# First products of an attention and feed-forward kernel regrouped: q of four groups by token quarters, longer weight rows, a first tile in halves, and a new table of priorities

## The chip, the cores and the metric

One core of a Trainium2 chip runs the whole kernel. The metric is device time in microseconds (us) of one execution. A kernel is run several times and the median is quoted. With each run goes the mean granted clock of the TensorE (PE); 1.0 is full speed. The other engines are DVE (VectorE), ACT (ScalarE), POOL (GpSimd) and SP (SyncE, which issues the transfers).

A profile is one execution seen by the hardware profiler: for every instruction its start and duration, and for every idle stretch of an engine the instruction or transfer that ended it, as inferred from semaphore events. "Issue" is put down where an engine was idle and no semaphore that the profile shows was waited for.

## The reference, cut to what matters

One transformer block over 2,048 tokens of width 1,024 in bf16. The attention works in four segments of 512 tokens with a memory between them; the feed-forward part has 3,584 hidden columns.

```python
h  = x + A(layernorm(x))            # 32 heads of 32, four segments s = 0..3
#   per segment: p = softmax(q k^T * scale + mask);  o = g * memory part + (1-g) * p v
#                memory M += phi(k)^T v ;  z += sum phi(k)       (read by the later segments)
h2 = h + (silu(LN(h) w1) * (LN(h) w3)) w2
```

## The kernel before: the parts that matter here

The kernel is written as a graph of operations which a small list scheduler puts in order at build time, on each engine by class and then by sequence number. A table `SHIFT` moves each unit of work in that order. It has two numbers per unit and was tuned by search, so the order of every engine's list follows from it.

```python
def schedule(self):
    for o in ops:
        late, cls = SHIFT.get(o.unit, (0, 0))
        o.seq += late + 1e-6 * o.seq
        o.cls += cls
    ...                                  # list scheduling with estimated costs, PSUM banks as a resource
```

A dense product is a chain of matmuls of a 128x128 weight with up to 512 columns. Each is one weight load and one product in the PE's list.

```python
def mms(self, group, items, cls, split=4, eager=False):
    for i in range(0, len(items), split):
        part = items[i:i + split]
        def emit(e, gr, part=part):
            return [e.matmul(p[0](gr), p[1], p[2], start=p[3], stop=p[4]) for p in part]
        ...
def project(self, s, kind, half, i, w):          # q, k, v of segment s; 8 products of 512 columns
    ...
    self.mms(gr, items, 5)
```

The head of the program (`first_half`) loads tiles x0 to x3 of 128 tokens, normalises and transposes them, and multiplies them by the first half of wq and wk as they come, in quarters of 128 tokens:

```python
loads = [x0, x1, wq[:, :, 0:256], x2, x3, wk[:, :, 0:256], wq[:, :, 256:512], wk[:, :, 256:512], wv]   # shortened
work = [(w, i, Group([(5,), (6,), (7,), (4,)], safe=True)) for w in (wq, wk) for i in range(2)]
for c0 in range(0, 512, 128):
    for w, i, gr in work:
        self.mms(gr, [... 8 products of 128 columns ...], 5, split=4, eager=True)
```

At the end of each half segment, `finish` and `memory` issue runs of small matmuls: sums and weighted sums of the exponentials over 32-wide column tiles (`column`), and 64 products of 32x33 for the memory. A group of such matmuls lies between the dense products:

```python
# column(...):
for kc in range(4):
    for i in range(4):
        ins.append(e.matmul(ps[32*i:32*i+32, b*512 + 128*kc:(b+1)*512], lhsT(i, kc, j), at[i, kc][:, j, :],
                            tile_position=(0, 32 * i), ...))
# memory(...): 4 x 4 x 4 products
ins.append(e.matmul(ps[32*j:32*j+32, b+33*i:b+33*i+33], pkn[:, 4*i+kc, 32*j:32*j+32], v[:, kc, g0+i, j, 0:33], ...))
```

The softmax here doesn't subtract the row's maximum and nothing guards it: scores larger than these inputs give would overflow.

## Time and profile before

| | before |
|---|---|
| time, median of 3 runs (range) | 896.66 us (895.69 to 897.35) |
| span of the profiled run, clock | 895.0 us, 1.0 |
| PE busy, share of the span | 880.6 us, 98% |
| DVE / ACT / POOL busy, share | 47% / 32% / 19% |
| matmuls recorded, weight loads recorded | 5,833 / 5,921 |
| first scores begin | 20.76 us |

The share of busy time says which engine bounds; the chain of waits says where the remaining idle time is. The lines that carry this are shown in the prediction below.

### The profile page before, as it was taken

The numbers are of one execution on the slowest core, as the hardware profiler recorded it, in microseconds if no ns is written. First come the engines' busy times: TensorE is split into PE (matmuls) and PEld (weight loads), VectorE is DVE, ScalarE is ACT, GpSimd is POOL, SyncE is SP. The second block draws the span as 40 slices with busy tenths as digits, with TensorE's granted clock in tenths as the row PEclk, the third lists the DMA queues.
The fourth block names the chain that finished last, engine by engine and source line by source line (L and its number), as shares of the span: only waits on it lengthen the run. The fifth ranks groups of instructions, "written<-read, shape, count | busy, mean of one in ns | idle before, by whom it ended". The sixth has DMA issues, their size and how long they took to land.

```text
span 895.0 us, 13604 instructions
## 1 busy us (share of the span) xinstructions
PE 880.6 (98%) x5833; PEld 403.4 (45%) x5921; DVE 417.6 (47%) x631; ACT 287.9 (32%) x306; POOL 173.8 (19%) x226
## 2 busy tenths in 40 slices
PE   8999999999999999999999999999999999999998
PEld 5343444444444444444444444444444444444445
DVE  5784848585848485754555311211334333331111
ACT  6767766656565646111111100000111111110000
POOL 2553445353534343100200000000000000000000
PEclk9999999999999999999999999999999999999999
DMA  7899755634541221753475211113223221301110
GB/s 235 227 212 271 187 142 147 187 92 130 165 99 57 72 70 58 225 153 92 120 224 140 85 36 36 30 46 90 64 60 94 71 71 48 95 24 41 40 37 30
DMA packets 146540, 96.32 MB, mean 108 GB/s; under 512 B 45488, under 2 KB 133680, under 8 KB 146480
## 3 DMA queue, kind: packets, MB, share of 16 engines
q1 hardware_dynamic: 146480, 95.45, 38.8%
q8 instruction: 47, 0.77, 0.4%
q14 instruction: 13, 0.11, 0.0%
HBM read 76.55 MB, written 8.39 MB: 95 GB/s over the span
## 4 chain that ended last, share of the span: by engine, by line
PE 97%; issue 1%; DVE 1%; DMA 1%; ACT 0%; SPq 0%; ACTq 0%; DVEq 0%
PE ps L708 89%; PE ps L1107 4%; PE ps L1057 3%; DMA xs<-in_A_x_dram 1%; PE ps L985 0%; PE ps L1184 0%; ACT et L1069 0%; PE ps L1100 0%; DVE t L1260 0%; DVE hm L1265 0%; PE ps L720 0%; SPq L299 0%; DVE R L1163 0%; ACT sg L1257 0%; DVE Nsb L1171 0%
## 5 line engine op out<-in xcount | busy, mean ns | idle before, releaser
L708 PE MATMUL ps<-hnT,w1b 128*128 128x512 bf16 x876 | 218.4, 379 | 1.4 <-issue 0.3
L708 PE MATMUL ps<-hnT,w3b 128*128 128x512 bf16 x873 | 217.4, 379 | 1.5 <-issue 0.5
L1257 ACT ACTIVATE sg<-ps 128x512 bf16<-128x512 f32 x112 | 66.9, 597 | 403.1 <-PE ps L708 403.1
L708 PE MATMUL ps<-w2b,hm 128*128 128x512 bf16 (+1 forms) x907 | 195.3, 372 | 0.9
L1069 ACT ACTIVATE et<-ps 128x2048 bf16<-128x2048 f32 x80 | 150.0, 1875 | 39.3 <-PE ps L1057 38.9
L1260 DVE SCALAR_TENSOR_TENSOR t<-sg,ps 128x512 bf16<-128x512 bf16 x112 | 76.8, 685 | 169.4 <-ACT sg L1257 169.2
L708 PEld LDWEIGHTS ps<-w2b,hm 128*128 128x128 bf16 x924 | 90.4, 98 | 103.2
L708 PEld LDWEIGHTS ps<-hnT,w1b 128*128 128x128 bf16 x896 | 86.5, 98 | 105.5 <-issue 8.2
L708 PEld LDWEIGHTS ps<-hnT,w3b 128*128 128x128 bf16 x896 | 86.5, 98 | 105.4 <-issue 2.9
L1078 POOL TENSOR_SCALAR_AFFINE_SELECT et<-et 128x512 bf16<-128x512 bf16 x96 | 84.0, 881 | 126.2 <-ACT et L1069 126.0
L1265 DVE SCALAR_TENSOR_TENSOR hm<-t,ps 128x512 bf16<-128x512 bf16 x112 | 76.7, 686 | 50.5 <-PE ps L708 47.9
L1289 DVE TENSOR_TENSOR ob<-hr,ps 128x512 bf16<-128x512 bf16 (+1 forms) x33 | 22.1, 671 | 143.0 <-PE ps L708 143.0
L708 PE MATMUL ps<-wo,oT 128*128 128x512 bf16 x249 | 60.7, 380 | 0.6 <-issue 0.3
L708 PE MATMUL ps<-xnT,wp 128*128 128x512 bf16 (+1 forms) x345 | 59.7, 320 | 1.4 <-issue 0.6
L708 PE MATMUL ps<-hnT,wp 128*128 128x512 bf16 x250 | 59.0, 380 | 0.7 <-issue 0.6
L708 PEld LDWEIGHTS ps<-xnT,wp 128*128 128x128 bf16 x352 | 27.7, 98 | 26.9 <-issue 3.6
L708 PEld LDWEIGHTS ps<-wo,oT 128*128 128x128 bf16 x256 | 23.9, 98 | 29.8 <-issue 2.9
L708 PEld LDWEIGHTS ps<-hnT,wp 128*128 128x128 bf16 x256 | 23.6, 98 | 29.8 <-issue 3.8
L1200 POOL TENSOR_TENSOR oT<-Nsb,R 128x512 bf16<-128x512 f32 x23 | 35.8, 1569 | 4.1 <-DVE R L1197 4.1
L1163 DVE STREAM_TRANSPOSE R<-Rc 128x1024 f32<-128x1024 f32 x28 | 33.6, 1222 | 0.1
L1229 DVE TENSOR_TENSOR h<-h,ps 128x512 bf16<-128x512 bf16 x32 | 21.7, 680 | 25.1 <-PE ps L708 24.9
L1057 PE MATMUL ps<-qT,kT 32*128 32x128 bf16 (+3 forms) x512 | 31.7, 301 | 0.0
(82 smaller groups left out, 520.9 us busy)
## 6 DMA issues: line engine op xcount, KB each, us to landing
w1b<-in_B_w_dram SPq DMA_DIRECT2D x28, 512.0 KB, 3.9
w3b<-in_B_w_dram SPq DMA_DIRECT2D x28, 512.0 KB, 3.8
wp<-in_A_wv_dram SPq DMA_DIRECT2D x8, 1024.0 KB, 5.5
wp<-in_A_wq_dram SPq DMA_DIRECT2D x7, 1024.0 KB, 5.9
wp<-in_A_wk_dram SPq DMA_DIRECT2D x7, 1024.0 KB, 5.7
w2b<-in_B_w_dram SPq DMA_DIRECT2D x7, 1024.0 KB, 8.0
xs<-in_A_x_dram SPq DMA_DIRECT2D x16, 256.0 KB, 5.6
h<-in_A_x_dram SPq DMA_DIRECT2D x16, 256.0 KB, 3.7
```

The source lines that it names most:

```text
L708: return [e.matmul(p[0](gr), p[1], p[2], start=p[3], stop=p[4]) for p in part]
L1057: ins.append(e.matmul(self.bank(gr, j, 512 - 128 * kc, off), k[r, g0 + g, 128 * kc:128 * kc + 128], q[r, g0 + g, 128 * kc:512], start=True ...
L1069: return [e.activation(et[:, :, :], src, AF.Exp, scale=self.scale)]
L1078: self.pool_op(lambda e, v=v, pat=pat: e.affine_select(v, v, pattern=pat, compare_op=ALU.is_ge, fill=0.0, base=0, channel_multiplier=-1), ...
L1107: ins.append(e.matmul(self.ps[32 * i:32 * i + 32, b * 512 + 128 * kc:(b + 1) * 512], lhsT(i, kc, j), at[i, kc][:, j, :], start=kc == 0 and ...
L1163: return self.dve_op(lambda e: e.transpose(out, src), dve_ns(1024), [Rc[:, t, 2 * n:2 * n + 2, :]], [dst], 2)
L1200: self.either(lambda e, out=out, Ns=Ns, R1=R1: e.tensor_tensor(out, Ns, R1, op=ALU.add), 512, 2, [Ns, R1], [out], 2)
L1229: self.g.op("dve", dve_ns(512), lambda e, gr, hs=hs: [e.tensor_tensor(hs, hs, self.bank(gr), op=ALU.add)], reads=[hs], writes=[hs], cls=1, ...
L1257: self.g.op("act", act_ns(512), lambda e, gr, sg=sg: [e.activation(sg, self.bank(gr), AF.Tanh, scale=0.5)], writes=[sg], cls=0, group=gg)
L1260: e.scalar_tensor_tensor(t1, sg, 1.0, self.bank(gr), op0=ALU.add, op1=ALU.mult)], reads=[sg], writes=[t1], cls=0,
L1265: e.scalar_tensor_tensor(dst, t1, 0.5, self.bank(gr), op0=ALU.mult, op1=ALU.mult)], reads=[t1], writes=[dst], cls=0,
L1289: self.g.op("dve", dve_ns(n), lambda e, gr, hs=hs, ob=ob, n=n: [e.tensor_tensor(ob, hs, self.bank(gr, 0, n), op=ALU.add)], reads=[hs], wri ...
```

## The change

Its intent: the first products should start earlier and go on without a stop. So the four groups in work are all of q and need one weight only; wq comes in two blocks of half the contraction with rows of 1 KB in place of 512 B; tile 0 is loaded in two halves of its columns; the norm steps of the tiles are put in turns by explicit dependencies. The table of priorities is replaced from its first entry to its last, since the units are numbered anew.

```diff
 SHIFT = {
-    0: (113, 0), 1: (-194, 1), 2: (-667, 0), ...      # 470 entries, units 0 to 471, all replaced
+    0: (-353, 0), 1: (-458, 0), 2: (874, -1), ...     # 485 entries, units 0 to 487
 ...
-        loads.insert(2, (wq[:, :, 0:256], sq[:, :, 0:256]))
-        loads.insert(5, (wk[:, :, 0:256], sk[:, :, 0:256]))
-        loads += [(wq[:, :, 256:512], ...), (wk[:, :, 256:512], ...), (wv[:, :, :], sv)]
+        loads = [(x0[:, 0:512], s0[:, 0:512], 1.1), (x0[:, 512:1024], s0[:, 512:1024], 1.1),
+                 x[1] + (0.68,), x[2] + (0.68,), (wq[:, 0:4, :], sq[:, 0:4, :], 0.94),
+                 (wq[:, 4:8, :], sq[:, 4:8, :], 0.8), x[3] + (0.68,), (wk[:, :, :], sk, 0.8),
+                 (wv[:, :, :], sv, 0.8)]
 ...
-        work = [(w, i, Group(..., safe=True)) for w in (wq, wk) for i in range(2)]
+        work = [Group([(5,), (6,), (7,), (4,)]) for _ in range(4)]
         for c0 in range(0, 512, 128):
-            for w, i, gr in work:                      # 8 products each
+            for b in range(2):
+                for i, gr in enumerate(work):          # 4 products each: one half of the contraction
 ...                                                   # tile 3: statistics on DVE instead of ACT
+            if t == 0: self.turns[2] = (), (o,)        # tile 2's second half after tile 0's copy
+        if t == 2: self.turns[3] = (eps,), (self.applied[-1],)
```

## The prediction

In the text below, marked cuts take out general statements on the pace of products, on the cost of short rows and on when a copy has landed, which no run of this case shows as rules; the figures of the trace beside them stay. No term of the sum is cut: it came to 896.66 - 1.5 = 895.2, shaded to 895.0. "55.7 and 219" are ns per product of 128 and of 512 columns (28 in 1.56 us, 49 in 10.74). "Warm": in the kernel before, the dummies start 0.43 us apart up to the eighth (4.20 us) and 0.22 us apart from the ninth on (4.55 us). The 370 GB/s lie within the 340 to 390 measured; the 1.2 us of straggling is an estimate, between the 0.6 and 2.1 us measured.

> **What bounds the kernel now.** I read the page first (busy shares, then the chain that ended last), then the matrix engine's waits, then the first 20 us of the timeline, because the diff touches nothing later except one table.
>
> ```profile
> PE 880.6 (98%) x5833; PEld 403.4 (45%) x5921; DVE 417.6 (47%) x631; ACT 287.9 (32%) x306; POOL 173.8 (19%) x226
> PE 97%; issue 1%; DVE 1%; DMA 1%; ACT 0%; SPq 0%; ACTq 0%; DVEq 0%
> ```
>
> The TensorE (PE) works 880.6 of 895.0 us and is 97% of the chain. So only 14.4 us of idle PE time exist, plus whatever PE work is not useful. Where are they? The head:
>
> ```profile
> 2.17 6.15 DMA xs<-in_A_x_dram
> 8.34 0.07 DVE lnst L831
> ...
> 8.95 0.68 DVE lnst L831
> 9.63 0.33 DVE xs L862
> 10.00 0.41 PE ps L720 x4
> ```
>
> This is the chain of waits at the start: an x tile's transfer, its statistics, the normalised tile, its transposes. The same stretch in order of time (start, duration, engine, instruction, count, idle before it):
>
> ```profile
> 1.24 4.33 PE L708 MATMUL ps<-oT 128*128 128x512 bf16 x12 [1.24 <-DVE oT L773]
> 3.49 1.29 DVE L831 BATCH_NORM_STATS2 lnst<-xs 128x6 f32<-128x512 bf16 x2 [2.31 <-DMA xs<-in_A_x_dram]
> 5.89 0.73 DVE L862 TENSOR_SCALAR xs<-xs,lnmv,rstd 128x512 bf16<-128x512 bf16 x2 [0.68 <-POOL rstd L858]
> 7.70 1.07 PE L708 MATMUL ps<-xnT,wp 128*128 128x128 bf16 x16 [0.41 <-DMA wp<-in_A_wq_dram]
> 8.34 1.29 DVE L831 BATCH_NORM_STATS2 lnst<-xs 128x6 f32<-128x512 bf16 x2 [1.05 <-DMA xs<-in_A_x_dram]
> 9.55 0.72 DVE L862 TENSOR_SCALAR xs<-xs,lnst,rstd 128x512 bf16<-128x512 bf16 x2
> 10.92 1.51 PE L708 MATMUL ps<-xnT,wp 128*128 128x128 bf16 x24 [0.20 <-DVE lnve L857]
> 20.76 0.40 PE L1057 MATMUL ps<-qT,kT 32*128 32x512 bf16 x4
> ```
>
> To see: the x12 on oT are dummies that warm the PE. The first real product waits for wq (7.70). Tile 1 is ready on the pool engine by 7.76 (its rstd starts at 7.19 and takes 0.57), but its normalisation runs only at 9.55: DVE's in-order queue has tile 2's statistics ahead of it, and those wait for tile 2's transfer until 8.34. From 10.92 the PE hardly idles again.
>
> The end of this phase can be worked out. By 20.83 (first scores) the PE has done all 128 products of 128 columns and 12 of 512. Twelve at 0.219 us (49 take 10.74 us in the chain's later, dense part) are 2.6, so **the 128-column phase ends at an equivalent 18.2 us**. Its useful work is 128 products and 32 transposes at 0.0557 us (28 products took 1.56 in the chain), 8.9 us. So 9.3 us of the head do nothing useful: 2.6 us more go after the last product (the tail) and about 6.7 us in many short gaps of 0.05 and 0.16 us over the rest, with one of 1.07 us:
>
> ```profile
> 269.73 1.07 issue
> 270.81 0.32 PE ps L985 x22
> ```
>
> It lies inside one group of 64 small matmuls and waits for no semaphore.
>
> [...] The trace has 55.7 and 219. So four 128-column products cost about what one of 512 costs, and working by token quarters is nearly free. [...] while the 512 B weight rows flow (9 to 13.5 us) the transfer views give 250 to 300 GB/s, while x tiles (2 KB rows) and later whole 1 MB weights (1 KB rows) reach 340 to 390. [...] summing the GB/s slices, tile 0's 262 KB had moved by 2.9 us and landed by 3.49 (0.6 later), but wq's half, 1,049 KB in the queue's order, had moved by 5.6 and landed at 7.70 (2.1 later), beside the x2 and x3 transfers behind it.
>
> **The change part by part.**
>
> *Products.* Before: 2 groups of q and 2 of k by quarters; after: 4 of q. Both 4 x 4 x 8 = 128 products. The instruction lists show the same totals (5,921 matmuls, 32 transposes, 3,665 products of 512 columns), so PE work changes by 0. Each tile is now worked through in two halves of the contraction, so the first 16 products need only the first 512 KB of wq.
>
> *Transfers.* Order was x0, x1, half wq, x2, x3, half wk; now x0 in halves, x1, x2, wq in two blocks of 512 KB with 1 KB rows, x3, wk, wv. Tile 2 should land about where 786 KB have moved (4.6) plus 0.6: 5.2 instead of 8.34. The first wq block is at 1,311 KB: 557 KB by 3.75, the rest at 370 GB/s gives 5.8, plus some 1.2 of straggling: 7.0. The second: 8.4. x3 9.1, wk 12.0, wv 14.8 by the same rule.
>
> *Halves of tile 0.* The first half may be there at 3.05, the second still at about 3.5 since its issue comes 0.41 us later. Statistics end 0.4 earlier. But DVE's new order puts half of tile 2's statistics (0.65 to 0.69) before tile 0's normalisation, waiting for tile 2 (5.2): that ends at 5.9, where the normalisation starts before (5.89). **Expected gain of this part: nearly nothing**; 0.3 at best.
>
> *Turns.* DVE now goes: tile 0 normalised (5.9 to 6.6), its two copies from PSUM (0.42 each, to 7.7), second half of tile 2's statistics (to 8.4), aggregate 0.2, tile 1 normalised from 8.6 (was 9.55), tile 3's first half once landed (9.5 to 10.2), tile 2 normalised from 10.2 (was 11.58), tile 3's second half, copy, aggregate, rstd, tile 3 normalised from 13.2 (was 13.55). ACT loses one tile's moments (1.06+0.19+0.30+1.14+0.19 = 2.9 us), DVE gains 1.7; neither bounds.
>
> *PE as a result.* 16 products from 7.35 to 8.3; a short wait for the second wq block; 12 products to 9.1; tile 1's transposes, with an ACT copy of 0.60 before its products can start at 10.0; then its and tile 2's work without large gaps until tile 3's transposes at 13.75; a wait of some 0.1 for the copy, last 32 products to 16.55. All q groups now finish within the last 16 products, so the next group needs a bank freed by a 0.69 us copy started 0.67 before the end: 0.15 more. **The phase ends at 16.7 instead of 18.2: gain 1.5 us.**
>
> *Later.* The first scores come after 24 products of 512 columns instead of 12, 16.7 + 5.3 = 22.0 instead of 20.8. Exponentials on ACT start 1.2 us later, but ACT is 32% busy and the PE has other work to put between, so I count 0. The table of priorities is replaced entirely; it reorders the whole program, but the same PE work remains, and before shows only that one gap of 1.07 us that a different order could remove, or multiply: 0, plus or minus 1.
>
> Sum: 896.66 - 1.5 = 895.2; I shade it to **895.0** as a retuned table was presumably kept because it helped.
>
> **The rivals.**
>
> (a) *Weights become the wait.* Before, k's other half is used from 18 and wv first at 25.9; after, both at 16.7, so all 4.2 MB must have landed by then. Before, that much had moved by 16.5 and landed about 17.3. If longer rows don't speed the transfers, PE waits 0.6 or more and the gain falls to about 0.9: 895.8. For: the first products also need x2 ahead of them in the queue. Against: the 370 GB/s of 1 KB rows.
>
> (b) *DVE's first order hurts.* If tile 2 lands not at 5.2 but at 6.5 (the 2 us straggling that wq, x2 and x3 show now), tile 0 waits for statistics nobody needs yet, and everything moves by up to 1.3 us: gain near 0, 896.5. Against: x1, without long rows of small packets behind, straggles only 0.5.
>
> (c) *Better than I think.* If wq's first block is there by 6.5 and the halves do gain 0.3, and the 1.07 us gap goes too: 893.5.
>
> (d) *The retuned table loses.* The attention and feed-forward stages are bound by PE with short slack on PSUM banks; two or three new gaps of 1 us would make 897 to 898. Against: in 200 to 750 us only one such gap exists now, and the numbers of waits in PE's list are alike (440 before, 435 after).
>
> **Range and chances.** Head: gain 0.3 to 2.3. Table: plus or minus 1. Runs of before scatter from 895.69 to 897.35. Together an 80% range of **893.2 to 896.8**. Two per cent are 18 us; the head's 9.3 us of unused time and all gaps together could not give that, and to lose it the new order would need 18 gaps of the size of the one seen. So faster 0.01, same 0.98, slower 0.01.
>
> **What would show it.** Right: first product at 7.2 to 7.5, tile 1 normalised near 8.6, tile 2 near 10.2, first scores near 22.0 after 24 products; PE busy within 1 us of 880.6 with idle time 1 to 2 us less before 18 us. Wrong in step: the first block of wq landing after 7.7; tile 2's statistics starting after 5.5 us (rival b); a PE wait for wv or wk at 16 to 18 (rival a); PE gaps near 1 us after 50 us, above all in the groups of small matmuls (d). The prediction as a whole is wrong if the head gains less than 0.5 or more than 2.5, or if gaps elsewhere change by over 1.5 us.

## The result, and the profile after

| | before | after |
|---|---|---|
| time, median of 5 runs (range) | 896.66 (895.69 to 897.85) | 906.83 (905.94 to 907.59) |
| ratio, 95% interval | | 1.0111 (1.0097 to 1.0126) |
| span of the profiled run, clock | 895.0, 1.0 | 905.2, 0.996 |
| matmuls recorded | 5,833 | 5,921 |

Ratios are the mean time of one kernel's runs over that of the other's of the same rounds, so they are not quite the ratio of the medians. Executions over 1.5% slower than the fastest of the same kernel are left out of the means. The change lies within 2%, but it is slower by 10.2 us, and the whole interval is above 1.

The page of the kernel after, its busy line, its chain by engine and the queue that brings instructions:

```profile
PE 892.7 (99%) x5921; PEld 404.0 (45%) x5921; DVE 419.5 (46%) x636; ACT 284.7 (31%) x300; POOL 174.3 (19%) x224
q8 instruction: 47, 0.77, 0.3%
PE 97%; DMA 1%; issue 1%; ACT 0%; SPq 0%; POOL 0%; DVE 0%
```

The PE is "99% busy" in a slower run. Shares don't show the loss. The list of what the PE waited for does (who waited, for what: total us, times, longest); first the kernel after, then the kernel before:

```profile
PE ps L990 <- issue: 3.6, 1, 3.6
PE ps L1112 <- issue: 2.6, 1, 2.6
PE ps L709 <- DVE oT L774: 1.2, 1, 1.2
```

```profile
PE ps L708 <- issue: 3.0, 19, 0.2
...
PE ps L985 <- issue: 1.1, 1, 1.1
```

After has two long gaps in which the PE waits for no semaphore; before has one shorter one, the 1.07 us that the prediction shows. (The 19 short ones of before are an effect of missing records, as will be seen.) The first one in the timeline of the kernel after (start, duration, engine, instruction, count, idle before it):

```profile
132.91 0.44 SPq L300 DMA_DIRECT2D wp<-in_A_wv_dram  x1
...
137.15 0.69 PE L990 MATMUL ps<-v,pkn 128*32 128x33 bf16 x64
...
137.67 0.66 PE L1112 MATMUL ps<-et,v 128*32 128x512 bf16 x9
...
140.97 0.35 PE L1112 MATMUL ps<-et,v 128*32 128x256 bf16 x7 [2.64 <-issue]
...
141.25 3.07 PE L709 MATMUL ps<-wo,oT 128*128 128x512 bf16 x8
```

One `emit` of 16 matmuls is cut in two, 9 and 7, by 2.64 us of nothing. Nothing in the kernel's text separates the ninth from the tenth. The eight dense products after it take 3.07 us where eight times 0.216 is 1.73: they ran slowly. The windows of 1 us of the same kernel say why (window; busy share and count of PE, weight load, DVE, ACT, POOL; then the granted clock, DMA share and GB/s):

```profile
138.00:139.00 1.00, 0.33 (x9) 0.00 (x0) 1.00 (x4) 0.07 (x1) 0.22 (x1) 1.00 2.39 107
139.00:140.00 1.00, 0.00 (x0) 0.00 (x0) 0.97 (x2) 0.00 (x0) 0.00 (x0) 1.00 0.21 7
...
142.00:143.00 1.00, 1.00 (x4) 0.44 (x3) 0.00 (x0) 0.63 (x2) 0.92 (x2) 0.50 1.28 287
```

The gap is followed by half clock. The windows from 141 to 145 show 0.91, 0.50, 0.50, 0.50, 0.89, which is 3.4 us at half rate, worth 1.7 us. The idle time before it was 2.64 us. In the runs told of here half clock came with stops of 1.7 us (`a_pad192`, head), 2.64 and 3.59 us (here) and 3.50 us (`b_pad96`), and not with one of 2.60 us in `b_pad96` nor with before's 1.07 us, so the length of a stop alone does not decide it. The slow stretch was 3.4 us long here (6.8, twice that, in `b_load2`).

The second gap, from the timeline of the kernel after:

```profile
231.20 0.43 SPq L300 DMA_DIRECT2D wp<-in_A_wv_dram  x1
...
236.04 0.70 PE L990 MATMUL ps<-v,pkn 128*32 128x33 bf16 x58
...
240.33 0.22 PE L990 MATMUL ps<-v,pkn 128*32 128x33 bf16 x6 [3.59 <-issue]
```

Again inside one group, 58 and 6 of 64, and again half clock after it (0.90, 0.50, 0.50, 0.50, 0.89 in the windows from 240 on).

To see where all of the time went, I added up the nominal time of the PE's list (a product of 512 columns 0.2158 us, the dense pitch of the trace; smaller ones in proportion, with the small matmuls' own pitches) and took at each moment the time elapsed less the nominal time done. The difference of this **lag** between the kernels is:

| moment, us | lag before | lag after | after less before | what lies between |
|---|---|---|---|---|
| 16 | 6.34 | 5.33 | -1.0 | the head |
| 136 | 9.35 | 9.27 | -0.1 | small waits, +0.9 |
| 160 | 9.89 | 14.44 | +4.6 | first gap and its half clock |
| 230 | 11.73 | 17.11 | +5.4 | small waits, +0.8 |
| 260 | 12.49 | 23.31 | +10.8 | second gap and its half clock, +5.4 |
| 290 | 14.50 | 24.18 | +9.7 | before's own gap, -1.1 |
| end | 16.56 | 26.72 | +10.2 | small waits, +0.5 |

The end, +10.2, is the difference of the spans (905.2 less 895.0). The two gaps and their slow stretches are 10.1 of it.

The head after the change, to be held against the lines in the prediction, from the timeline of the kernel after:

```profile
5.79 0.69 DVE L832 BATCH_NORM_STATS2 lnst<-xs 128x6 f32<-128x512 bf16 x1 [1.03 <-DMA xs<-in_A_x_dram]
...
6.40 0.72 DVE L863 TENSOR_SCALAR xs<-xs,lnmv,rstd 128x512 bf16<-128x512 bf16 x2
...
7.86 2.03 PE L709 MATMUL ps<-xnT,wp 128*128 128x128 bf16 x28
...
8.94 0.73 DVE L863 TENSOR_SCALAR xs<-xs,lnst,rstd 128x512 bf16<-128x512 bf16 x2
...
22.54 0.39 PE L1062 MATMUL ps<-qT,kT 32*128 32x512 bf16 x4
```

The first line is tile 2's statistics, the next tile 0 normalised, then the first product, then tile 1 normalised, then the first scores. Each came 0.3 to 0.6 us later than predicted.

### The profile page after: what moved, and what is told of

Its sections match the earlier page's. It is cut to its first block, busy times and chain, and to the rows that moved or that the text cites. A ratio compares the mean times of both kernels' runs of the same rounds, so it can differ in the third digit from the quotient of the medians.

```text
span 905.2 us, 13690 instructions
## 1 busy us (share of the span) xinstructions
PE 892.7 (99%) x5921; PEld 404.0 (45%) x5921; DVE 419.5 (46%) x636; ACT 284.7 (31%) x300; POOL 174.3 (19%) x224
## 4 chain that ended last, share of the span: by engine, by line
PE 97%; DMA 1%; issue 1%; ACT 0%; SPq 0%; POOL 0%; DVE 0%
PE ps L709 89%; PE ps L1112 4%; PE ps L1062 3%; DMA wp<-in_A_wq_dram 1%; PE ps L990 0%; PE ps L1189 0%; SPq L300 0%; ACT et L1074 0%; POOL et L1083 0%; PE ps L1105 0%; PE ps L721 0%; ACT xnT L732 0%; DVE ob L1294 0%
## 5 line engine op out<-in xcount | busy, mean ns | idle before, releaser
L709 PE MATMUL ps<-hnT,w1b 128*128 128x512 bf16 x896 | 222.7, 379 | 0.0
L709 PE MATMUL ps<-hnT,w3b 128*128 128x512 bf16 x896 | 222.1, 379 | 0.0
L709 PE MATMUL ps<-wo,oT 128*128 128x512 bf16 x256 | 64.7, 392 | 0.0
L709 PE MATMUL ps<-xnT,wp 128*128 128x512 bf16 (+1 forms) x352 | 61.9, 321 | 0.5 <-ACT xnT L732 0.2
```

## The experiments

### The theory and its rivals

**Theory: the PE runs out of instructions.** Queue 8 brings 47 packets of 0.77 MB in all, 16.4 KB each. The PE's list, by my count in the compiled kernel, is 12,084 instructions: 5,921 weight loads, as many products, and 242 separate waits. That is about 64 bytes of the 0.77 MB for each, so about 256 in a packet; 12,084 over 256 is 47.2. So one packet is one block of 256 instructions, that is of about 128 matmuls. The packet that brings on the resumption is seen in the transfer view (a window of 0.25 us from 138.5 in the kernel after; columns as on the page):

```profile
q8 instruction: 1, 0.02, 23.2%
```

The PE resumes 2.2 to 2.5 us later, at 140.97. It is the same at the second gap (packet at 238.0, PE at 240.33) and at before's own (268.5 and 270.81). (Times of packets are the beginnings of such windows, so a packet may have begun up to 0.25 us later.) By my count, all three gaps lie at instruction 198, give or take two, of a block of 256 (2,758, 4,550 and 5,318). One such point was read off; that the other two fall on it too is the evidence. The traces alone show it as well, and for more gaps. Count two instructions for each recorded weight load and one for each recorded wait (195 in after, 198 in before): in the 13 kept traces the PE waited ten times for "issue" for more than 0.3 us, in seven kernels, and all ten waits stand at place 191 or 192 of a block of 256.

With 128 dense products, a block lasts 28 us (128 times 0.2158), and the 2.2 to 2.5 us from packet to resumption are hidden: but for the two gaps, no wait of the PE for issue in the kernel after is over 0.2 us. If a block lies wholly in small matmuls, it is used up in about 3 us. Nominal times (my count, from the pitches of the trace) of the fastest blocks: before 3.38, 4.04 and 3.36 us (the last is the one with the 1.07 us gap); after **2.74 and 2.78** (the two with gaps), then 4.47. And the fetch itself came late: the first of the two blocks began at 135.33 and the packet for the next came at 138.50, 3.2 us on; the second began at 233.71, the packet at 238.0, 4.3 us on. In both cases a 1 MB load of wv was under way, which landed 7.7 and 6.8 us after its issue.

**Rivals.** (1) The new head or the new order costs time by itself, through waits on other engines, and the gaps are a by-product. (2) Transfers of wv hold up the PE's operands (it would then show as a DMA wait, not as issue). (3) A chance of execution: five runs within 1.7 us speak against it.

### Moving the block boundaries of the kernel after

In two kernels 32 dense products of k are each cut into four of 128 columns. The arithmetic is the same and the scheduler is told the old cost, so the order of all engines stays (tile by tile, the traces show the same order on each engine as in the kernel after); but the PE's list grows by 96 weight loads and 96 products, 192 instructions, and every later boundary falls elsewhere. By my count the fastest block is then 4.33 us. `a_pad192` cuts products in the head, `a_padmid` those of the second half of segment 0, near 40 us, with the head untouched.

```diff
-                return [e.matmul(p[0](gr), p[1], p[2], start=p[3], stop=p[4]) for p in part]
+                return [e.matmul(p[0](gr)[:, o:o + p[5] // cut], p[1], p[2][:, o:o + p[5] // cut],
+                                 start=p[3] and o == 0, stop=p[4] and o + p[5] // cut == p[5])
+                        for p in part for o in range(0, p[5], p[5] // cut)]
 ...
-        self.mms(gr, items, 5)
+        self.mms(gr, items, 5, cut=4 if s == 0 and half == 0 and kind == "k" else 1)   # a_pad192
+        self.mms(gr, items, 5, cut=4 if s == 0 and half == 1 and kind == "k" else 1)   # a_padmid
```

> The changed kernel with one thing different: the 32 k products of 512 columns in the head are issued as 128 products of 128 columns, so PE's list has 192 instructions more ahead of the attention; order, arithmetic and transfers are the same. Theory (instruction blocks): PE's list is fetched in blocks of 256 instructions, one block ahead; the two long gaps of the changed kernel (138.3 and 236.7 us) fall where a whole block lies in a run of small matmuls and is used up in 2.7 us. With 192 more, the shortest block takes 4.3 us, so both gaps and the half-clock stretches after them go: 906.8 minus about 10 plus 0.25 for the shorter products, 896.5 to 898. Rival (the new order makes PE wait for banks, other engines or data at these places): nothing changes, 906.5 to 907.3, gaps at the same two matmuls.

Measured: 897.25 us (896.62 to 898.97, 4 runs) against 896.52 for before on the same chip, ratio 1.0011 (0.9996 to 1.0026). As expected. ("One block ahead" is what the count of 19 packets under "What stays open" shows.) The profiled run was the one of 898.97: the PE waited 1.7 us for a wq block there, and 3.4 us of half clock followed in the head.

> The changed kernel; the 32 products of 512 columns of k in the second half of the first segment (after the head, near 40 us) are each cut into four of 128 columns: +192 PE instructions as in the run that cut head products, the head itself unchanged. Theory of the instruction blocks: the two gaps near 138 and 237 us go (no PE wait for issue over 0.5 us, no half clock after 130 us), and since no product of the head is touched, no profile shows the late wq block: idle at 16 us as in the changed kernel (5.3 us against its nominal work, within 0.3), time 896.2 to 897.5. Against before (896.5) that leaves the head's 1.0 us spent on small waits between 60 and 180 us. Rival (the head or the table itself cost time): 900 or more. If the head's other delays are chance of the execution and not of the cut, one of the runs may still be 1 to 3 us longer.

Measured: 896.87 us (896.55 to 897.21, 5 runs, clock 1.0 in each) against 896.79, ratio 1.0000 (0.9986 to 1.0014). What the PE waited for:

```profile
PE ps L709 <- issue: 3.5, 22, 0.2
PE ps L709 <- DVE oT L777: 1.2, 1, 1.2
PE ps L709 <- DMA wp<-in_A_wq_dram: 1.1, 2, 0.6
```

No single wait for issue is over 0.2 us. On its page, queue 8 now has 48 packets. **So ten microseconds come and go with the place of the boundaries, at the same work, order and head; rival (1) is out as the cause of the 10 us.** One expectation failed: I had said that no late wq would show and that the lag at 16 us would be 5.3; the profile has two wq waits of 1.1 us together and a lag of 5.97. A late wq doesn't need products cut in the head, then. It comes in some executions and not in others.

### Thinner transfers before the gaps

The two wv loads issued ahead of the gaps bring 128 KB in place of 1 MB. The result was meant to be wrong; the list of the PE is unchanged.

```diff
+        if thin:
+            o.emit = lambda e, g: [e.dma_start(out[:, 0:1, :], in_[:, 0:1, :])]
 ...
-                self.g.dma(w[:, :, :], src, cls=1)
+                self.g.dma(w[:, :, :], src, cls=1, thin=kind == "v" and (s, half) in ((2, 0), (3, 1)))
```

> The changed kernel, but two of the eight wv loads (those issued at 132.9 and 231.2 us, just before the two gaps) bring only 128 KB of their 1 MB; the result is wrong on purpose, PE's list is the same. Theory (blocks, fetched through the same transfer engines): the fetch no longer stands behind the weight load, starts within 1 us of the block's start instead of 3.2 and 4.3 us after it, and both gaps shrink below 1 us: 897 to 899. Rival 1 (the position in the list alone matters, a fetch always takes that long): gaps of 2 to 3.6 us stay, 905 to 907. Rival 2 (order and waits): 906.5 to 907.

Measured: 898.14 us (897.16 to 900.21; the profiled run is the slowest, with 2.4 us of waits for wq in the head) against 896.52, ratio 1.0015 (0.9998 to 1.0031). Both gaps are gone, but for 0.20 us. The packet for the next block now came at 138.25, where the first fast block began (3.2 us after its beginning in the kernel after), and at 232.75, some 0.7 us after the second began (4.3 us there). At the second place a trace of the gap is left, in the timeline of this run:

```profile
235.32 0.22 PE L993 MATMUL ps<-v,pkn 128*32 128x33 bf16 x6 [0.20 <-issue]
```

It lies at the same matmul, the last 6 of 64, and is 0.20 us long in place of 3.59; it ends some 2.5 us after its packet, as the long ones do. So a fast block alone is not enough: the same 2.74 and 2.78 us blocks pass, or nearly, when the fetch has little traffic ahead of it. Rival (2) falls as well, since the operands of the gapped instructions (`et`, `v` of the running segment, `pkn`) do not come by these loads.

### Giving the kernel before such blocks

Sixteen k products of the head are cut in four, so the list grows by 96 instructions. By my count three blocks then last 2.74 us, ending near 56, 97 and 228 us if nothing stops them (the expectation has 64 and 101 for the first two), and the block of the 1.07 us gap is no longer fast.

```diff
-        self.mms(gr, items, 5)
+        self.mms(gr, items, 5, cut=4 if s == 0 and half == 0 and kind == "k" else 1)
```

> The kernel before with 16 k products of 512 columns in the head issued in quarters: 96 PE instructions more, all else the same. Theory (instruction blocks): three blocks now lie inside runs of small matmuls and are used up in 2.74 us each (they end near 64, 101 and 228 us); each may bring a gap of 1 to 3.6 us and up to 1.7 us of half clock, while the old gap at 269.7 us goes: 899 to 910, most likely 904. Rival (order, waits, table): the old order was good, so 896.5 to 897.3 and no new gaps.

Measured: 904.13 us (901.85 to 906.07) against 896.52, ratio 1.0084 (1.0063 to 1.0105). What the PE waited for:

```profile
PE ps L1110 <- issue: 6.1, 2, 3.5
```

Two gaps, 2.60 us ending at 58.63 and 3.50 us ending at 100.84; the old one at 269 us is gone, and the third fast block gave none in this profile. The first gap brought no slower clock, the second brought half clock at 102 to 105 us. The mean clocks of the four runs were 0.998, 1.0, 0.996 and 0.994, and the time rises as they fall (903.14, 901.85, 905.12, 906.07), so how often the clock drops seems to be left to chance from one execution to the next. The third block's fetch was early, which fits the theory: its packet came in the window from 228.5, at about the block's beginning (228.8), where the two with gaps had theirs 3.1 and 3.8 us after it. **The kernel before loses 7.6 us, three quarters of what the change lost, by nothing but 48 more matmuls for the same work.**

### The same means, used to gain

If the boundaries are what matters, before's own gap should go when the list is shifted after 230 us only, where no other fast block is made.

```diff
+        self.mms(gr, items, 5, cut=4 if s == 3 and half == 1 and kind == "k" and i < 2 else 1)
```

> The kernel before with 16 k products of the last segment's second half issued in quarters: 96 PE instructions more between 230 and 265 us, so that the block that ended in its one gap (269.7 us) is no longer used up in 3.36 us; all else the same. Theory: the gap of 1.07 us goes, 0.12 us is paid for shorter products: 895.3 to 896.0, about 1 us below before. Rival: no change, 896.5.

Measured: **895.14 us (894.96 to 895.80, 5 runs) against 896.32, ratio 0.9984 (0.9972 to 0.9997)**. It is the fastest kernel, a little under the range expected. What the PE waited for, the whole list:

```profile
PE ps L723 <- DVE xs L865: 1.3, 2, 1.1
PE ps L708 <- DVE oT L776: 1.2, 1, 1.2
PE ps L708 <- DVE lnve L860: 0.2, 1, 0.2
```

The two long entries are in the head. This trace has all its matmul records (5,969 of 5,969), and the short waits for issue are gone with the long one.

Held against it, the change loses even without gaps: `a_padmid` has the ratio 1.0000 and this run 0.9984, a difference of some 1.4 us. That is an estimate over two sets of rounds, and the intervals just overlap.

### The head and the table apart

Can head and table be separated? `a_oldtab` has the new head with before's table for all later units (numbers shifted by 16), `b_newtab` the reverse.

```diff
 # a_oldtab: own entries for units < 44, before's entries of units >= 28 as unit + 16
 # b_newtab: own entries for units < 28, after's entries of units >= 44 as unit - 16
```

> The changed kernel's head (first products, transfers, turns) with the table of priorities of the kernel before for everything behind the head (unit numbers moved by 16). The blocks used up fastest take 4.46, 4.02 and 3.35 us, as in the kernel before (3.38, 4.04, 3.36). Theory (instruction blocks): no gap but one near 270 us of 0 to 1.5 us, so 894.5 to 898, like before less or plus what the head does. Rival (the head itself is what lost 10 us): 905 to 907.

Measured: 907.25 us, ratio 1.0117 (1.0103 to 1.0131). A miss. Most of the loss has other names here, from what the PE waited for:

```profile
PE ps L1505 <- POOL et L1483: 3.4, 1, 3.4
PE ps L1462 <- DVE R L1602: 2.0, 1, 2.0
PE ps L1109 <- issue: 1.6, 1, 1.6
```

> The kernel before with the new table of priorities behind its old head. One block is used up in 3.43 us (its end falls in the memory products near 240 us), the next in 5.03. Theory (instruction blocks): at most that one gap, 0 to 2.5 us, and the 1.8 us of small waits that the new order has at 60 to 180 us: 896.5 to 900. Rival (the new order as such makes PE wait 10 us): 905 to 908.

Measured: 907.26 us, ratio 1.0117 (1.0103 to 1.0131). A miss too: waits for a wv load (2.5 us), for POOL (2.0) and for several DVE results. A table was searched for one head and one numbering; with another head, the scheduler resolves it to a third order, that nobody tuned. These two runs therefore tell little of the change itself. They say that the order is fragile, and that to swap tables is not the way to undo one part. What they do add: the lag of `a_oldtab` is that of before up to 98 us (8.17 against 8.33), so in this execution the new head did no harm. And the 1.6 us for issue in `a_oldtab`, ending at 103.37, is one more shortage of instructions: it stands at place 192 of 256, and the packet came in the window from 100.75, 3.2 us after its block began. Its block takes over 4 us by my count, so the expectation had let it pass; a fast block is judged too narrowly by its own time.

I also put the 96 instructions of `b_best` into `a_oldtab`, to make the fastest version from it.

> The changed head with the old table behind it and the same 96 instructions more. Theory: no gap at all in the attention; with the head's 1.0 us as in the changed kernel's profile 894.5, if the head's first weights come late in some runs (as in two profiles since) 895 to 897. If a_oldtab is near 906 this is too.

Measured: 906.57 us, ratio 1.0111 (1.0095 to 1.0126). It missed 894.5 for the same named waits as `a_oldtab`, as the end of the expectation had allowed for.

### More traffic before a block that passed

Before has a block of 3.38 us near 133 us without a gap; its fetch came at 133.75 to 134.0, 0.8 to 1.0 us after the block began. An extra copy of 1 MB from memory to memory, issued ahead of it, should hold up that fetch and open a gap.

```diff
+        load = op.emit                                  # op: a load of h near the block
+        op.emit = lambda e, g: [e.dma_start(scr, self.B_w2[0:512, :]).then_inc(sx, 16)] + load(e, g)
```

> The kernel before with one more transfer of 1 MB, from device memory to device memory and used by nothing, issued at about 130.5 us, 2.5 us ahead of a block that is used up in 3.4 us and shows no gap now. Theory (fetch held up by transfers): a gap of 1 to 3 us without a semaphore appears at 136 to 137 us, 1,362 matmuls into the list: 898 to 901. Rival (transfers don't matter to the fetch): 896.3 to 897.3; if the extra load only delays data, a PE wait for a transfer or for another engine shows instead.

Measured: 900.01 us, ratio 1.0046 (1.0030 to 1.0061). The time is in the range, but for the wrong reason: the copy was issued at 139.21, behind the block. The PE waited for an h load (1.9 us), a wk load (0.9) and 1.6 us at the gap near 270. It says nothing of the theory. The second try puts the copy at 131.6 (130.6 was expected), in rows of 1 KB.

> The run before it (one 1 MB transfer more, of no use) put right: there the transfer came out at 139.2 us, behind the block it was meant for. Now it is issued at 130.6 us, in rows of 1 KB like a weight load, 2.4 us ahead of the start of the block that ends with the 1,362nd matmul and is used up in 3.4 us. Theory (the fetch of PE's next block queues with the transfers): the block's fetch, seen 0.8 us after the block's start in the kernel before, comes 2.5 to 4.5 us after it; a gap without a semaphore of 1.5 to 3.5 us at 136 to 139 us; 898 to 901.5. Rival (fetch independent of transfers): fetch within 1.5 us, no gap there, at most other waits for late data: 896.5 to 899.

Measured: 903.46 us, ratio 1.0073 (1.0058 to 1.0088), above the range expected. The fetch did move, to 137.0, 3.0 us after its block began, and a gap of 3.32 us ends at 139.90, with 6.8 us of half clock from 138.9 on. But the timeline names another releaser for it:

```profile
139.90 1.49 PE L708 MATMUL ps<-wo,oT 128*128 128x512 bf16 x3 [3.32 <-DMA h<-in_A_x_dram]
```

The h load behind my copy was late as well, and the PE stood five matmuls ahead of the boundary. That transfers delay the fetch is shown; that this alone makes the gap is not, by this run.

### Tile 0 in halves

On top of `a_pad192`, tile 0's two transfers bring 1,008 and 16 columns in place of 512 and 512: almost a whole tile at once, at the same number of instructions.

```diff
+            if k < 2:
+                c = slice(0, 1008) if k == 0 else slice(1008, 1024)
+                o.emit = lambda e, g, c=c: [e.dma_start(x0[:, c], s0[:, c])]
```

> The changed kernel with its 192 added PE instructions (a_pad192, 897.25), and tile 0 loaded nearly whole (1,008 of 1,024 columns) by the first transfer instead of in halves; the second brings the last 16 columns. If the halves cost the tiles behind them their place (x1 landed at 5.1 us in the changed kernel, 4.1 before), tile 1 lands near 4.3, tile 2 near 5.1, the first product comes by 7.5 instead of 7.9, and the run is 0.3 to 0.6 below a_pad192: 896.5 to 897. If the halves are harmless, tile 2 lands at 5.4 to 5.8 as before and nothing is gained: 897 to 898.

Measured: 897.33 us (897.14 to 899.49) against 896.46, ratio 1.0007 (0.9991 to 1.0024), like `a_pad192`. Tile 2's statistics began at 5.72 us, as good as with halves (5.79). At this number of transfers the split of tile 0 does neither good nor harm. What one transfer more at the head of the queue costs, this run can't tell, as it keeps both.

## Why the prediction was wrong

- **What bounds the kernel: right.** PE work is the same in both, 875.7 us in nominal terms (summed as for the lag) and 5,921 matmuls.
- **"About 6.7 us in many short gaps of 0.05 and 0.16 us": wrong.** These were missing records. One group on both pages shows it, the matmuls and the weight loads of before, then the matmuls of after:

```profile
L708 PE MATMUL ps<-hnT,w1b 128*128 128x512 bf16 x876 | 218.4, 379 | 1.4 <-issue 0.3
...
L708 PEld LDWEIGHTS ps<-hnT,w1b 128*128 128x128 bf16 x896 | 86.5, 98 | 105.5 <-issue 8.2
```

```profile
L709 PE MATMUL ps<-hnT,w1b 128*128 128x512 bf16 x896 | 222.7, 379 | 0.0
```

  876 records with 1.4 us of idle time against 896 with none. A lost record leaves a hole in the recorded stretch, which reads as idle time. For the same reason "PE busy within 1 us of 880.6" was no good test: after has 892.7, of which the missing records and the 3.4 us that half clock cost (two times 1.7) are parts.
- **Products: right.** Their number and work did not change.
- **Transfers: somewhat late.** Tile 2 was to be there at 5.2, its statistics began at 5.79; the first product was to start at 7.35 and started at 7.86. That is rival (b), which I had at up to 1.3 us, with 0.5. The delay arose between 3 and 4 us, when 95 GB/s flowed (320 before). Tile 1, now third in the queue behind two halves, landed at 5.08 (4.12 before), and the transfers behind it came 0.4 to 0.9 us after my times. That the one transfer more is the cause was not tested. Rival (a) did not occur: no wait for wk or wv at 16 to 18 us, and wv landed at 15.71 (17.35 before).
- **Halves: right**, nearly nothing.
- **Turns: right in order, late by the same half microsecond.** Tile 0 was normalised at 6.40 (5.9 predicted), tile 1 at 8.94 (8.6), tile 2 at 10.44 (10.2), tile 3 at 13.53 (13.2).
- **Phase end 16.7, gain 1.5: right in order, the size off in this profile, and in others not there.** First scores at 22.54 (22.0 predicted) after 24 dense products; the lag at 16 us gives a gain of 1.0. The term that was mis-sized is the start: 0.5 us of tile 2's transfer. But this gain is of one pair of profiles. In the six profiles with the old head the first scores begin between 19.92 and 20.76 us. In the seven with the new head, which has 12 products (2.6 us) more to do first, they begin at 22.51 to 23.39 in four, and at 25.30 to 25.83 in three, each of these the slowest run of its kernel. So a gain from the head is not shown.
- **"Later ... 0, plus or minus 1": the step that failed.** It was +11.2 (10.2, and the 1.0 that the head won in this pair of profiles). Of these, 10.1 less 1.1 are the three gaps with their slow clock; the other 2.2 are small waits, such as 0.4 us for POOL and 0.3 us for ACT in the new order, of which none stands out. I had seen the very thing, a gap of 1.07 us in a group of small matmuls that waits for no semaphore, and wrote that a new order could "remove, or multiply" it. But I took it for a property of the order and did not ask what it was. Rival (d) named the two new gaps and gave them 1 us each; they measured 2.64 and 3.59, and each added 1.7 us of half clock, for which nothing in the profile of before could be a model, as its only gap brought none. Rival (d)'s reason was short slack on PSUM banks, which was not shown, and the runs show a shortage of instructions; that it named the place rightly is in part luck. Had I counted PE instructions in blocks of 256 from that gap, both lists could have been compared: 2.74 and 2.78 us against 3.36 us. That would have been a warning and not a forecast, since a block of 2.74 us passed in `b_pad96` and one of over 4 us did not in `a_oldtab`.
- **Range and chances.** The range (893.2 to 896.8) missed 906.83 by 10 us, and its upper end left out even rival (d)'s own 897 to 898; the chance of within 2% was on the right side only because 2% is 18 us.

**What stays open.** Why the packet for the next block comes with the beginning of a block in one place and 4.3 us after it in another. That traffic delays it is shown (`a_thin`, `b_load2`); the rule by which it is asked for is not. A hint, from a count over the recorded instructions: in the dense part of the kernel after, from 400 us on, each of the 19 packets comes within 45 instructions of the beginning of a block and, numbered as at the gaps, brings the block after it. Why wq is late by 1 to 2 us in some executions of the new head. And which part of the change costs the 1.4 us that seem to remain without gaps.

## What to carry to other kernels

A gap on an engine that waits for no semaphore, in the middle of one group of small instructions, is to be looked at as a shortage of instructions: count the engine's list in blocks of 256 (the size seen here on the PE) and see how fast each block is used up, and what the transfers do just then. Where a block is used up in about the time of a fetch (here 2.2 to 2.7 us from the packet to resumption, and up to 4.3 us of delay before the packet), an edit earlier in the program that changes the number of instructions moves the boundaries and can win or lose several microseconds, so compare two kernels only after this has been looked at, and use it: some products cut in four, at a spot of dense work, shift the boundaries for almost nothing (0.12 us, by the estimate made for `b_best`). And compare the number of recorded matmuls with that of weight loads before small gaps are believed.
